# Attention, soft mixture of experts and MLP on one core: slot sums through a scaled stacking matrix, other early chunks of w_out, and single quarter copies of g

## The chip, the core and the metric

One Trainium2 chip, one core of it. The metric is the device time of one execution in microseconds (us). Engines: PE (TensorE), DVE (VectorE), ACT (ScalarE), POOL (GpSimd), SP (SyncE, which here issues the DMAs).

## What is computed

```python
attn_out = _attn_ref(q, k, v)            # 4 batches, 8 heads, 576 tokens, 64 wide; q and k rotated
x = attn_out.transpose(0, 2, 1, 3).reshape(2304, 512)
# soft mixture of experts, 32 slots
logits = x @ phi
d = exp(logits - logits.max(0)); d /= d.sum(0) + 1e-09     # over the tokens
slot_input = (d.T @ x).reshape(8, 4, 512)
for e in range(8):
    h = np.maximum(slot_input[e] @ w1[e], 0.0)             # 512 -> 1024
    slot_out[e] = h @ w2[e]                                # 1024 -> 512
c = exp(logits - logits.max(1)); c /= c.sum(1) + 1e-09     # over the slots
x = c @ slot_out
# MLP
h = x @ w_in                                               # 512 -> 2048
g = h * (1.0 / (1.0 + np.exp(-h)))
return g @ w_out                                           # 2048 -> 512
```

All of it is float32; matmuls of float32 go over PE in passes, or as sums of products of a high part and a low part (`_hi`, `_lo`).

## The kernel before

The work stands in four stages. Attention takes 16 pairs of heads one after the other. The mixture of experts keeps, while attention runs, a running slot sum `s_b` over the first three batches of tokens. The last batch is taken in two halves of 256 and 320 tokens: `half(0)` and `half(1)` return lists of functions (logits, maximum, exp, transposes, slot sums, merges), and the driver calls these, `h0[...]` and `h1[...]`, in an order written out by hand. `x_15(1)` transposes the last piece of x for the logits of half 1 (PE L414 and L416, ACT copy `xt` L418). Logits of half 1 come as four groups `lgh1` of eight passes (L514).

At the end of attention `sc` holds the factors by which older sums shrink when the maximum grows (ACT L538). The upper 64 rows of `s_b` are scaled on ACT (L539), the lower 64 are merged with the new sums on DVE (`merge` L568; two instructions of `slots`, L574). `slots` then multiplies `s_b` by the stacking matrix `stack_i`, which adds up the groups of 32 rows, into `si_ps` (PE L580) and copies it to `si` (DVE L581), in two rounds of 256 columns. Five small DVE operations make the slots' denominators `den`. The transposed logits `lt` (PE L842, DVE copies L844 and L845) serve the weights over slots. Layer 1 multiplies `si` by w1 (L871, 32 matmul groups of four for each half of its columns) and layer 2 by w2 (L892); the tiles `w` of both are loaded by SP. `slot_t(g)` copies a half of layer 2's result to SBUF as `o` (ACT L902) and transposes it to `so`.

The MLP folds w_in into the slots: `g_product(n)` multiplies `so` by a quarter of w_in (L1089; for the first columns L1126), and `gs` holds the result g spread over four groups of rows, as high and low parts. For n = 1 to 3 the spreading is done by `g_copy(n, r)`, r = 0 to 3, with four copies of 32x128 each; `ACT_QUADRANTS` says which of the four go to ACT (L1103), and the rest go to DVE (L1105). `hidden(j, k)` makes chunk k (128 columns of the 2048) for block j (768 of 2304 tokens): two matmuls `hps` (PE L1049), a sigmoid (ACT L1053), the product (DVE L1056), the high part `ghi` (ACT L1059) and the low part `glo` (DVE L1062). The products follow: for each of 3 blocks, 16 chunks and 6 groups of tokens three matmuls `ops` (L1154 to L1156).

The chunks of w_out arrive as 64-bit words and are narrowed to 32 bits by three instructions (ACT L134, DVE L137, DVE L140), then split into `wo_hi` (ACT L1031) and `wo_lo` (POOL L1032, or DVE where the call says so). Four chunks, `W_OUT_EARLY`, are loaded and narrowed during attention into `wf_early`. Of the others, 0 and 1 come ahead of the first products (tiles `wf_first`, `hw_first`), the rest within the products.

Order: all up to the split of chunk 1 is written out by hand under `tc.manual_schedule()`. Behind it, the framework's scheduler places the instructions, from the order of the code as a start. In the products, a table of steps (`G_STEPS`, step = 6 k + token group) says after which group of products the g products, copies and last conversions of w_in stand. The DMAs issued on SP take turns over 8 semaphores, and each waits for the landing of the eighth before it.

## Time and profile before

| | us |
|---|---|
| median of 3 runs | 573.48 (572.96 to 574.97) |
| the profiled execution | 573.27 |
| its span | 571.5 |
| PE busy | 540.4 (95%) |
| DVE busy | 316.9 (55%) |
| ACT busy | 307.9 (54%) |
| POOL busy | 111.3 (19%) |
| mean granted clock of PE | 0.982 |

The time is the span and 1.8 us around it. Times in rows are us from the start of the span. Attention ends at about 300, layers 1 and 2 run to 338, the MLP from there to the end. In a row of the timeline, the first number is the start, the second the duration (first to last end for a group), then engine, line, operation, what it writes and reads, sizes, and the count; in brackets stands how long the engine had been idle, and the instruction that ended that. The granted clock is given as a share of full speed.

### The profile page before, as it was taken

Reading aid. Unit: us, or ns where it says so; the run is one execution under the profiler, and the core shown is the slowest. Engines: PE = TensorE matmul, PEld = TensorE weight load, DVE = VectorE, ACT = ScalarE, POOL = GpSimd, SP = SyncE. Lnnn points to the kernel's source line nnn. Section 1 sums busy time; section 2 is a strip of 40 time slices with the busy share of each in tenths; the row PEclk is TensorE's granted clock in tenths of the full one; section 3 lists DMA queues with packets and bytes.
Section 4 is the critical chain, followed back from the end, with each engine's and each line's share of the span. In section 5 each row is a group of like instructions: output and inputs, shape, how many; then the busy total and the mean of one; then the engine's idle time right before and its main releaser. Section 6 shows DMA issues by size and latency. Waiting matters only on the chain.

```text
span 571.5 us, 15141 instructions
## 1 busy us (share of the span) xinstructions
PE 540.4 (95%) x6219; PEld 438.1 (77%) x6219; DVE 316.9 (55%) x841; ACT 307.9 (54%) x612; POOL 111.3 (19%) x96
## 2 busy tenths in 40 slices
PE   5599999999999999999979989899999999999997
PEld 2378989898897998888853337677888888888885
DVE  4756666766666567654130457697454444544442
ACT  2366667666767566664421327987554433544332
POOL 4933332313333323200000021133000000000000
PEclk9679999999999999999998999999999999999999
DMA  8226777635665575743799895422020000200003
GB/s 301 95 56 206 266 244 278 203 116 172 224 231 172 207 265 166 249 166 107 296 322 382 306 359 179 135 93 75 0 93 18 1 1 1 96 16 0 2 0 111
DMA packets 36773, 88.70 MB, mean 155 GB/s; under 512 B 10560, under 2 KB 11872, under 8 KB 34784
## 3 DMA queue, kind: packets, MB, share of 16 engines
q1 hardware_dynamic: 36694, 87.73, 44.3%
q8 instruction: 49, 0.80, 0.6%
q14 instruction: 20, 0.16, 0.1%
q10 hardware_dynamic: 10, 0.00, 0.0%
HBM read 78.20 MB, written 7.60 MB: 150 GB/s over the span
## 4 chain that ended last, share of the span: by engine, by line
PE 76%; ACT 10%; DVE 5%; DMA 4%; issue 3%; POOL 1%; SPq 1%; ACTq 0%; DVEq 0%
PE u L386 10%; PE ops L1156 10%; PE ops L1154 10%; PE ops L1155 10%; PE st L353 8%; PE psmx L300 3%; PE st_r L366 3%; PE l L871 3%; PE hps L1049 3%; ACT e L357 3%; PE xps L414 3%; DMA w_out_raw<-in_w_out_dram 2%; PE psmx L316 2%; ACT relu L308 2%; PE u L380 2%
## 5 line engine op out<-in xcount | busy, mean ns | idle before, releaser
L1056 DVE TENSOR_TENSOR hps<-hps,g 128x384 f32<-128x384 f32 x96 | 49.8, 561 | 84.6 <-ACT g L1053 84.3
L1053 ACT ACTIVATE g<-hps 128x384 f32<-128x384 f32 x96 | 42.3, 490 | 82.3 <-PE hps L1049 81.9
L1154 PE MATMUL ops<-wo_hi,ghi 128*128 128x512 f32 x216 | 84.7, 392 | 0.0
L1155 PE MATMUL ops<-wo_lo,ghi 128*128 128x512 f32 x216 | 84.4, 391 | 0.0
L1156 PE MATMUL ops<-wo_hi,glo 128*128 128x512 f32 x216 | 84.3, 390 | 0.0
L321 DVE CUSTOM_DVE_ANT_0 relu<-psmx,relu 128x288 f32<-128x288 f32 x140 | 57.7, 455 | 47.1 <-ACT e L357 36.3
L357 ACT ACTIVATE e<-st 128x512 f32<-128x512 f32 (+1 forms) x128 | 76.4, 650 | 10.9 <-PE st L353 10.9
L386 PE MATMUL u<-v,e 128*64 128x65 f32 x2048 | 80.6, 225 | 0.0
L386 PEld LDWEIGHTS u<-v,e 128*64 128x64 f32 x2048 | 71.5, 139 | 6.2 <-issue 3.0
L308 ACT ACTIVATE relu<-psmx 128x576 f32<-128x576 f32 x62 | 40.1, 652 | 51.7 <-PE psmx L300 33.6
L259 POOL TENSOR_TENSOR raw<-raw,tab 128x576 f32<-128x576 f32 x29 | 41.8, 1442 | 132.8 <-DMA raw<-in_qk_dram 96.7
L1062 DVE TENSOR_TENSOR glo<-hps,ghi 128x384 fp32r<-128x384 f32 x96 | 49.4, 552 | 5.0 <-ACT ghi L1059 1.8
L1059 ACT ACTIVATE ghi<-hps 128x384 fp32r<-128x384 f32 x96 | 45.6, 494 | 10.2 <-DVE hps L1056 10.1
L1156 PEld LDWEIGHTS ops<-wo_hi,glo 128*128 128x128 f32 x216 | 40.6, 188 | 8.5
L1155 PEld LDWEIGHTS ops<-wo_lo,ghi 128*128 128x128 f32 x216 | 40.6, 188 | 7.5 <-issue 0.4
L1154 PEld LDWEIGHTS ops<-wo_hi,ghi 128*128 128x128 f32 x216 | 40.6, 188 | 7.5 <-issue 0.2
L256 POOL TENSOR_TENSOR raw<-raw,tab 128x576 f32<-128x576 f32 x29 | 42.0, 1447 | 0.0
L353 PE MATMUL st<-hi 64*128 64x256 f32 (+1 forms) x256 | 39.7, 302 | 0.0
L353 PE MATMUL st<-mq,neg_a 64*128 64x256 f32 (+1 forms) x256 | 39.1, 297 | 0.6 <-DMA mq<-m 0.6
L353 PE MATMUL st<-hi,lo 64*128 64x256 f32 (+1 forms) x256 | 38.9, 296 | 0.0
L353 PE MATMUL st<-lo,hi 64*128 64x256 f32 (+1 forms) x256 | 38.9, 296 | 0.0
L397 DVE TENSOR_SCALAR r<-u 128x4 f32<-128x4 f32 (+1 forms) x32 | 5.2, 164 | 49.7 <-PE u L388 30.1
(223 smaller groups left out, 998.7 us busy)
## 6 DMA issues: line engine op xcount, KB each, us to landing
w<-in_w_dram SPq DMA_DIRECT2D x64, 512.0 KB
raw<-in_qk_dram SPq DMA_DIRECT2D x14, 1152.0 KB
w_out_raw<-in_w_out_dram SPq DMA_DIRECT2D x16, 512.0 KB
w_in_raw<-in_w_in_dram SPq DMA_DIRECT2D x12, 512.0 KB
v<-in_v_dram SPq DMA_DIRECT2D x16, 325.0 KB
out_dram<-os SPq DMA_DIRECT2D x18, 256.0 KB
raw<-in_qk_dram SPq DMA_DIRECT2D x4, 576.0 KB
w_in<-w_in SPq DMA_DIRECT2D x8, 256.0 KB
```

Source lines behind the costliest of these rows:

```text
L308: act.activation(out=r, in_=pair[:, :, 0:HS], func=ACTF.Relu)
L321: dve.tensor_tensor_reduce(out=r[:, hd], in0=t[hd], in1=r[:, hd], scale=1.0, scalar=-3.0e38, op0=ALU.add, op1=ALU.max, accum_out=mxs[p % 2 ...
L353: pe.matmul(st[:, hd, 0:n], lhsT=a, rhs=b, start=i == 0, stop=i == 3, skip_group_check=True)
L357: act.activation(out=e[:, :, 0:n], in_=st[:, :, 0:n], func=ACTF.Exp, scale=0.125)
L386: pe.matmul(u[q:q + 64, 2 * i + hd], lhsT=e[:, hd, o:o + 64], rhs=x[:, hd], start=n == 0 and i + hd == 0, stop=n == 4, skip_group_check=True)
L1053: act.activation(out=g[i], in_=t[i], func=ACTF.Sigmoid)
L1056: dve.tensor_tensor(out=t[i], in0=t[i], in1=g[i], op=ALU.mult)
L1059: act.activation(out=ghi[:, i], in_=t[i], func=ACTF.Copy)
L1062: dve.tensor_tensor(out=glo[:, i], in0=t[i], in1=ghi[:, i].bitcast(F32), op=ALU.subtract)
L1154: pe.matmul(t, lhsT=a, rhs=wo_hi[k], start=k == 0, stop=False)
L1155: pe.matmul(t, lhsT=a, rhs=wo_lo[k], start=False, stop=False)
L1156: pe.matmul(t, lhsT=b, rhs=wo_hi[k], start=False, stop=k == 15)
```

## The change

At the end of attention, `x_15(1)` moves from behind half 0's transposes to behind the first group of `lgh1`. The older sums `s_b` are no longer scaled in place: DVE scales the stacking matrix (`ss` = `stack_i` times `sc`), PE multiplies `s_b` by it, and adds the product of the newest sums with the plain `stack_i` in the same accumulators. For that, the newest sums are copied from PSUM to SBUF in two halves of 256 columns, one on ACT and one on DVE. One copy of 128x128 takes the place of two for `si`. The `lt` copies go to ACT, their accumulator into another pool, and the denominators (`total`) come last. `slot_t` copies its `o` in halves too. In both places, DVE's half waits for a semaphore of ACT in the built program, and the instruction that raises it is ACT's half of the same copy.

The early chunks of w_out are 0, 3, 6 and 10 instead of 3, 6, 9 and 12. So chunk 0's load and narrowing vanish from the start of the MLP, and its `wo_lo` is made on DVE there; 9 and 12 are now narrowed within the products. Two groups of products of chunk 0 are issued ahead of `g_spread`. The quarters of g are copied each at a step of its own, two of four on ACT instead of three, and the steps of the second and third g product and of the last conversion move.

```diff
-W_OUT_EARLY = (3, 6, 9, 12)
+W_OUT_EARLY = (0, 3, 6, 10)
...
-G_STEPS = (5, 7, 16, 19, 28, 14, 23, 37, 46, 53, 58)
-ACT_QUADRANTS = (0, 1, 2)
+G_STEPS = (5, 22, 52)
+LOAD_STEP = 28
+CONV_STEPS = (14, 23, 37, 44)
+ACT_QUADRANTS = (0, 1)
...
                         act.activation(out=sc[:, 5:6], in_=mall[:, 1:2], func=ACTF.Exp, bias=nmb[:, 5:6])
-                        act.activation(out=s_b[0][64:128], in_=s_b[0][64:128], func=ACTF.Copy, scale=sc[64:128, 5:6])
+                        ps["ss"] = p_r.tile([128, 3, NSLOT], F32, tag="dh0", name="ss")[:, 0]
+                        dve.tensor_scalar(out=ps["ss"], in0=stack_i[:, 0:NSLOT], scalar1=sc[:, 5:6], scalar2=None, op0=ALU.mult)
...
-                def slots():
-                    acc = s_b[0]
-                    for j in range(2):
-                        w = slice(256 * j, 256 * j + 256)
-                        dve.scalar_tensor_tensor(out=acc[0:64, w], in0=acc[0:64, w], scalar=sc[0:64, 5:6], in1=ps["s"][0:64, w], op0=ALU.mult, op1=ALU.add)
-                    t2 = ps_mx.tile([128, 2, 512], F32, tag="mx", name="si_ps")
-                    for j in range(2):
-                        t = t2[:, j]
-                        for k in range(2):
-                            c0 = 256 * j + 128 * k
-                            pe.matmul(t[:, NSLOT * k:NSLOT * k + NSLOT], lhsT=acc[:, c0:c0 + 128], rhs=stack_i[:, 0:NSLOT], start=True, stop=True)
-                        dve.tensor_copy(out=si[:, 2 * j:2 * j + 2], in_=t[:, 0:64].rearrange("p (k s) -> p k s", k=2))
+                def slots(t):
+                    o = hb[1][0:64, 0:DM]
+                    act.activation(out=o[:, 0:256], in_=ps["s"][0:64, 0:256], func=ACTF.Copy)
+                    dve.tensor_copy(out=o[:, 256:512], in_=ps["s"][0:64, 256:512])
+                    for k in range(4):
+                        pe.matmul(t[:, NSLOT * k:NSLOT * k + NSLOT], lhsT=s_b[0][:, 128 * k:128 * k + 128], rhs=ps["ss"], start=k == 0, stop=False, skip_group_check=True)
+                    for k in range(4):
+                        pe.matmul(t[:, NSLOT * k:NSLOT * k + NSLOT], lhsT=o[:, 128 * k:128 * k + 128], rhs=stack_i[0:64, 0:NSLOT], start=False, stop=True, skip_group_check=True)
+                    dve.tensor_copy(out=si, in_=t[:, 0:4 * NSLOT].rearrange("p (k s) -> p k s", k=4))
+
+                def total():
                     dve.tensor_tensor(out=scs[:, 3:5], in0=sc[:, 3:5], in1=sb[:, 3:5], op=ALU.mult)
...
-            h1[0]((0, 1, 2))
+            h1[0]((0,))
+            x_15(1)
+            h1[0]((1, 2))
             assert not tasks, tasks
             h0[3]()
             h0[5]()
-            x_15(1)
             h1[0]((3,))
             h1[2]()
             h0[4]()
             h1[3]()
+            h0[6]()
+            h0[8]()
+            h1[5]()
             h1[4]()
-            h0[6]()
-            h1[5]()
-            h0[8]()
+            t = ps_mx.tile([128, 2, 512], F32, tag="mx", name="lt3_ps")
             h1[6]()
-            t = ps_st.tile([128, 2, 512], F32, tag="st", name="lt3_ps")[:, 0]
+            h1[7](t[:, 1])
...
-            h1[7]()
-            dve.tensor_copy(out=lt[:, 15:19], in_=t[:, 0:4 * NSLOT].rearrange("p (c s) -> p c s", c=4))
-            dve.tensor_copy(out=lt[0:64, 19], in_=t[0:64, 4 * NSLOT:5 * NSLOT])
+            act.activation(out=lt[:, 15:19], in_=t[:, 0, 0:4 * NSLOT].rearrange("p (c s) -> p c s", c=4), func=ACTF.Copy)
+            act.activation(out=lt[0:64, 19], in_=t[0:64, 0, 4 * NSLOT:5 * NSLOT], func=ACTF.Copy)
+            h1[9]()
...
-            act.activation(out=o, in_=op[g], func=ACTF.Copy)
+            act.activation(out=o[:, 0:256], in_=op[g][:, 0:256], func=ACTF.Copy)
+            dve.tensor_copy(out=o[:, 256:512], in_=op[g][:, 256:512])
...
-        load_wo(0)
...
-            for k in range(2):
-                first.append((t[:, k], narrow(raw_w.pop(k), t[:, k], None, None, hw=h[:, k])))
+            first.append((t, narrow(raw_w.pop(1), t, None, None, hw=h)))
...
-        (wf0, _), (wf1, n1) = first
+        wf1, n1 = first[0]
+        split_hl(0, wf_early[0], dve)
...
-        hidden(*seq[0], between=lambda: (split_hl(0, wf0, dve), g_product(0)))
+        hidden(*seq[0], between=lambda: g_product(0))
         n1[0]()
+        for i in range(2):
+            products(0, 0, i, *gt[0, 0])
         g_spread()
...
+    for n in range(1, 4):
+        put(G_STEPS[n - 1], lambda n=n: g_product(n))
         for r in range(4):
-            g_copy(n, r)
...
+            put(NI * (4 * n + r - 3) + 1, lambda n=n, r=r: g_copy(n, r))
+    put(LOAD_STEP, lambda: load_last(1))
+    for k, x in enumerate(CONV_STEPS):
+        put(x, lambda k=k: conv_last(k))
```

DVE at the end of attention, before: `dh1` is the copy that the last slot sums wait for, `sps3` and `sps5` are the new sums of the halves.

```order
L530 TENSOR_SCALAR nmb_81<-mb_80,mall_85 128x1
L554 COPY dh1_4862<-dps5_4911 128x96
L568 SCALAR_TENSOR_TENSOR s_b0_77<-sps3_4902,sc_83,s_b0_77 64x512
L574 SCALAR_TENSOR_TENSOR s_b0_77<-s_b0_77,sc_83,sps5_4918 64x256 x2
L581 COPY si_79<-si_ps_4943 128x64 x2
L582 TENSOR_TENSOR scs_84<-sc_83,sb_82 128x2
```

The same place now (`last_logits_4826` is the buffer that now takes the newest sums):

```order
L532 TENSOR_SCALAR nmb_81<-mb_80,mall_85 128x1
L542 TENSOR_SCALAR ss_4900<-cst_sb_73,sc_83 128x32
L571 SCALAR_TENSOR_TENSOR s_b0_77<-sps3_4902,sc_83,s_b0_77 64x512
L557 COPY dh1_4862<-dps5_4912 128x96
L576 COPY last_logits_4826<-sps5_4920 64x256
L581 COPY si_79<-lt3_ps_4919 128x128
L584 TENSOR_TENSOR scs_84<-sc_83,sb_82 128x2
```

`ss` and the merge moved ahead of `dh1`; one half copy and one `si` copy replace two merges and two copies.

DVE at the start of the MLP, before: the numbers after `hps0_`, `ghi0_` and `glo0_` are the chunk and the half of its tokens.

```order
L908 COPY so_5035<-otp1_5334 128x4x16
L137 TENSOR_SCALAR wf_first_5322<-hw_first_5323 128x512
L140 SCALAR_TENSOR_TENSOR wf_first_5322<-w_out_raw0_5212,wf_first_5322 128x512
L929 TENSOR_TENSOR gs0_5343<-g0_ps_5373,gs0_5343 64x128
L1056 TENSOR_TENSOR hps0_0_0_5397<-hps0_0_0_5397,g0_0_0_5401 128x384
L1056 TENSOR_TENSOR hps0_0_1_5399<-hps0_0_1_5399,g0_0_1_5404 128x384
L1032 TENSOR_TENSOR wo_lo0_5408<-wf_first_5322,wo_hi0_5407 128x512
L1062 TENSOR_TENSOR glo0_0_5396<-hps0_0_0_5397,ghi0_0_5395 128x384
L1062 TENSOR_TENSOR glo0_0_5396<-hps0_0_1_5399,ghi0_0_5395 128x384
L929 TENSOR_TENSOR gs0_5343<-g0_all_5435,gs0_5343 64x384
L137 TENSOR_SCALAR wf_first_5322<-hw_first_5323 128x512
L140 SCALAR_TENSOR_TENSOR wf_first_5322<-w_out_raw1_5217,wf_first_5322 128x512
```

The same place now:

```order
L907 COPY o1_5334<-l2_1_5240 128x256
L1033 TENSOR_TENSOR wo_lo0_5372<-wf_early_903,wo_hi0_5371 128x512
L913 COPY so_5038<-otp1_5337 128x4x16
L934 TENSOR_TENSOR gs0_5343<-g0_ps_5377,gs0_5343 64x128
L1057 TENSOR_TENSOR hps0_0_0_5401<-hps0_0_0_5401,g0_0_0_5405 128x384
L1057 TENSOR_TENSOR hps0_0_1_5403<-hps0_0_1_5403,g0_0_1_5408 128x384
L1063 TENSOR_TENSOR glo0_0_5400<-hps0_0_0_5401,ghi0_0_5399 128x384
L1063 TENSOR_TENSOR glo0_0_5400<-hps0_0_1_5403,ghi0_0_5399 128x384
L934 TENSOR_TENSOR gs0_5343<-g0_all_5443,gs0_5343 64x384
L139 TENSOR_SCALAR wf_first_5324<-hw_first_5325 128x512
L139 TENSOR_SCALAR wf2_5480<-hwo2_5481 128x512
L142 SCALAR_TENSOR_TENSOR wf_first_5324<-w_out_raw1_5218,wf_first_5324 128x512
```

Chunk 0's narrowing is gone from between `so` and `gs0`, its `wo_lo0` stands ahead of `so`, and a step of chunk 2 has come between the two steps of chunk 1.

ACT in the products, at the first g product of the four that are spread by copies, before: `gh1` and `gl1` are its high and low part.

```order
L1095 ACTIVATE gh1_5536<-g_ps1_5519 128x128
L1103 ACTIVATE gs0_5343<-gh1_5536 32x128 x2
L1103 ACTIVATE gs0_5343<-gl1_5537 32x128
L1103 ACTIVATE gs0_5343<-gh1_5536 32x128 x2
L1103 ACTIVATE gs0_5343<-gl1_5537 32x128
L1103 ACTIVATE gs0_5343<-gh1_5536 32x128 x2
L1103 ACTIVATE gs0_5343<-gl1_5537 32x128
L1103 ACTIVATE gs0_5343<-gh1_5536 32x128 x2
L1103 ACTIVATE gs0_5343<-gl1_5537 32x128
L1053 ACTIVATE g0_3_0_5573<-hps0_3_0_5571 128x384
L1053 ACTIVATE g0_3_1_5580<-hps0_3_1_5578 128x384
```

The same place now:

```order
L1096 ACTIVATE gh1_5536<-g_ps1_5519 128x128
L1054 ACTIVATE g0_3_0_5561<-hps0_3_0_5559 128x384
L1104 ACTIVATE gs0_5343<-gh1_5536 32x128 x3
L1054 ACTIVATE g0_3_1_5568<-hps0_3_1_5566 128x384
L1104 ACTIVATE gs0_5343<-gh1_5536 32x128 x2
L1060 ACTIVATE ghi0_3_5557<-hps0_3_0_5559 128x384
L1104 ACTIVATE gs0_5343<-gh1_5536 32x128
L1060 ACTIVATE ghi0_3_5557<-hps0_3_1_5566 128x384
L136 ACTIVATE hwo5_5650<-w_out_raw5_5489 128x512
L136 ACTIVATE hw3_1_5706<-w_in_raw3_0_5228 128x512
L1054 ACTIVATE g0_4_0_5615<-hps0_4_0_5613 128x384
L1032 ACTIVATE wo_hi4_5605<-wf4_5600 128x512
```

Twelve copies in a row became eight (six of them here), which stand in groups among the sigmoids and high parts of the next chunks.

## Rows read from the trace of the kernel before

**Rows 1.** The page, part 4: shares of the chain that ended last.

```profile
PE 76%; ACT 10%; DVE 5%; DMA 4%; issue 3%; POOL 1%; SPq 1%; ACTq 0%; DVEq 0%
```

**Rows 2.** Stretches: length, busy PE, PEld, DVE, ACT, POOL, granted clock, DMA share, GB/s.

```profile
296.70:300.60 3.90, 1.77 (x17) 1.42 (x14) 2.35 (x11) 0.00 (x0) 0.00 (x0) 1.00 0.76 237
300.60:304.90 4.30, 4.30 (x25) 1.42 (x29) 0.00 (x0) 0.00 (x0) 0.00 (x0) 0.60 1.04 393
301.50:304.60 3.10, 3.10 (x20) 1.04 (x16) 0.00 (x0) 0.00 (x0) 0.00 (x0) 0.50 1.06 404
323.00:340.00 17.00, 15.48 (x130) 6.25 (x126) 4.89 (x15) 3.49 (x9) 0.57 (x1) 1.00 1.02 395
373.00:400.00 27.00, 25.91 (x141) 20.75 (x141) 22.80 (x47) 20.80 (x48) 9.28 (x6) 1.00 0.25 79
```

**Rows 3.** Timeline, the logits of half 1 and the last transposes of x.

```profile
288.65 1.82 PE L514 MATMUL lgh<-xt,phi_sb 128*32 128x320 f32 x24
...
289.67 0.47 ACT L533 ACTIVATE last_logits<-lgh,nmb 128x256 f32<-128x256 f32 x1 [2.41 <-DVE mall L527]
...
291.46 0.44 ACT L418 ACTIVATE xt<-xps 128x320 f32<-128x320 f32 x1 [1.04 <-PE xps L416]
...
291.95 0.75 PE L514 MATMUL lgh<-xt,phi_sb 128*32 128x320 f32 x8 [0.54 <-ACT xt L418]
```

**Rows 4.** Timeline, a half copy on ACT, then the slot sums up to layer 1.

```profile
286.87 0.39 ACT L516 ACTIVATE last_logits<-lgh 128x256 f32<-128x256 f32 x1 [2.39 <-PE lgh L511]
...
294.12 0.28 ACT L538 ACTIVATE sc<-mall,nmb 128x1 f32<-128x1 f32 x1
...
294.86 0.26 DVE L554 COPY dh<-dps 128x96 f32<-128x96 f32 x1 [1.35 <-PE dps L552]
295.03 0.73 DVE L568 SCALAR_TENSOR_TENSOR s_b<-sps,sc,s_b 64x512 f32<-64x512 f32 x1
...
296.91 0.87 DVE L574 SCALAR_TENSOR_TENSOR s_b<-s_b,sc,sps 64x256 f32<-64x256 f32 x2 [1.14 <-PE sps L565]
...
300.60 0.64 PE L871 MATMUL l<-w,si 128*32 128x512 f32 x4 [1.58 <-DVE lt L845]
```

**Rows 5.** Timeline of layers 1 and 2: first matmuls, last weight loads, last matmuls.

```profile
300.60 12.20 PE L871 MATMUL l<-w,si 128*32 128x512 f32 x96 [1.58 <-DVE lt L845]
...
303.41 18.83 SPq L120 DMA_DIRECT2D w<-in_w_dram  x16
...
336.17 1.94 PE L892 MATMUL l<-w,ht 128*32 128x512 f32 x16
```

**Rows 6.** Timeline, the start of the MLP.

```profile
338.23 0.60 ACT L902 ACTIVATE o<-l 128x512 f32<-128x512 f32 x1 [5.27 <-PE l L892]
...
339.43 4.37 POOL L1032 TENSOR_TENSOR wo_lo<-wf_early,wo_hi 128x512 fp32r<-128x512 f32 x3 [22.65 <-DMA w_in<-w_in]
...
341.02 1.64 DVE L140 SCALAR_TENSOR_TENSOR wf_first<-w_out_raw,wf_first 128x512 uint32<-128x512 uint32 x1
342.69 0.29 DVE L929 TENSOR_TENSOR gs<-g_ps,gs 64x128 fp32r<-64x128 f32 x1
...
347.45 0.43 DVE L137 TENSOR_SCALAR wf_first<-hw_first 128x512 uint32<-128x512 uint32 x1
...
347.91 0.69 DVE L140 SCALAR_TENSOR_TENSOR wf_first<-w_out_raw,wf_first 128x512 uint32<-128x512 uint32 x1
...
350.63 0.39 PE L1154 MATMUL ops<-wo_hi,ghi 128*128 128x512 f32 x1
```

**Rows 7.** Timeline of the first stall; groups of 347 to 400 (count, busy, mean ns, idle).

```profile
361.77 0.45 PE L1049 MATMUL hps<-cs,gs 128*128 128x384 f32 x1 [1.16 <-DVE glo L1062]
...
L1049 PE MATMUL hps<-cs,gs 128*128 128x384 f32 x22 | 7.5, 370 | 2.4 <-DVE glo L1062 1.8 <-DVE gl L1096 0.5
L1103 ACT ACTIVATE gs<-gh 32x128 fp32r<-32x128 f32 x22 | 6.8, 309 | 0.3
...
L1105 DVE CAST gs<-gl 32x128 fp32r<-32x128 f32 x12 | 2.7, 222 | 0.2
```

More of the change, by code (lines that the diff above doesn't have):

```diff
@@ L586, in slots @@
                     dve.reciprocal(out=den, in_=den)
-                return logits, logits2, soft, expo, keep, d_t, s_mm, slots, merge
+                return logits, logits2, soft, expo, keep, d_t, s_mm, slots, merge, total
             CHUNKS = [[(128 * c, min(128, S - 128 * c)) for c in range(5)]] * 4
@@ L992, in t3 @@
             combine_t(3)
-            t, h = (wa.tile([128, 2, 512], F32, tag=f"w{i}", name=n) for i, n in ((3, "wf_first"), (4, "hw_first")))
-            for k in range(2):
-                first.append((t[:, k], narrow(raw_w.pop(k), t[:, k], None, None, hw=h[:, k])))
+            t, h = (wa.tile([128, 512], F32, tag=f"w{i}", name=n) for i, n in ((3, "wf_first"), (4, "hw_first")))
+            first.append((t, narrow(raw_w.pop(1), t, None, None, hw=h)))
         first = []
@@ L999, in attn_softmoe_mlp_kernel @@
         slot_t(1)
-        for f in first[0][1]:
-            f()
         gs2 = [spare(10, "gs0")]
@@ L1113, in attn_softmoe_mlp_kernel, with products @@
     seq = [(j, k) for j in range(NBLK) for k in range(16)]
+    ops = {}
+    def products(j, k, i, ghi, glo):
+        if k == 0:
+            ops[j, i] = ps_o.tile([128, DM], F32, tag="o", name=f"ops{j}_{i}")
+        t = ops[j, i]
+        a, b = ghi[:, 128 * i:128 * i + 128], glo[:, 128 * i:128 * i + 128]
+        pe.matmul(t, lhsT=a, rhs=wo_hi[k], start=k == 0, stop=False)
+        pe.matmul(t, lhsT=a, rhs=wo_lo[k], start=False, stop=False)
+        pe.matmul(t, lhsT=b, rhs=wo_hi[k], start=False, stop=k == 15)
     def dummy(n):
@@ L1136, in attn_softmoe_mlp_kernel, with put @@
     hidden(*seq[1])
-    def copies(n):
-        for r in range(4):
-            g_copy(n, r)
-    extra = {}
-    for x, f in zip(G_STEPS, (lambda: g_product(1), lambda: copies(1), lambda: g_product(2), lambda: copies(2), lambda: load_last(1),
-                              lambda: conv_last(0), lambda: conv_last(1), lambda: conv_last(2), lambda: conv_last(3), lambda: g_product(3), lambda: copies(3))):
-        extra.setdefault(divmod(x, 6), []).append(f)
-    ops = {}
+    extra = {}
+    def put(x, f):
+        extra.setdefault(divmod(x, NI), []).append(f)
+    for n in range(1, 4):
+        put(G_STEPS[n - 1], lambda n=n: g_product(n))
+        for r in range(4):
+            put(NI * (4 * n + r - 3) + 1, lambda n=n, r=r: g_copy(n, r))
+    put(LOAD_STEP, lambda: load_last(1))
+    for k, x in enumerate(CONV_STEPS):
+        put(x, lambda k=k: conv_last(k))
     for n, (j, k) in enumerate(seq):
@@ L1149, in attn_softmoe_mlp_kernel @@
         for i in range(NI):
-            if k == 0:
-                ops[j, i] = ps_o.tile([128, DM], F32, tag="o", name=f"ops{j}_{i}")
+            if (j, k, i) not in ((0, 0, 0), (0, 0, 1)):
+                products(j, k, i, ghi, glo)
             t = ops[j, i]
-            a, b = ghi[:, 128 * i:128 * i + 128], glo[:, 128 * i:128 * i + 128]
-            pe.matmul(t, lhsT=a, rhs=wo_hi[k], start=k == 0, stop=False)
-            pe.matmul(t, lhsT=a, rhs=wo_lo[k], start=False, stop=False)
-            pe.matmul(t, lhsT=b, rhs=wo_hi[k], start=False, stop=k == 15)
             if (n, i) in extra:
```

2 lines of the change are left out of this document (1 added, 1 removed).

## The prediction

> **What bounds the kernel now.** I read the chain of waits first: PE carries 76% of it, ACT 10%, DVE 5% [rows 1]. So the end moves only where PE waits or runs at a lower clock. The edit touches two places where that happens: the stretch between the last attention matmuls and layer 1, and the start of the MLP with its first products. Next I took busy time and granted clock by stretch. In 296.7 to 300.6 PE works 1.77 of 3.90 us. Right after that, in layer 1, the granted clock is 0.50 for 3.1 us, that is 1.2 GHz, and 0.60 on the mean over 300.6 to 304.9, where PE has no gap at all [rows 2]. Then I went through the timeline at the end of attention [rows 3, 4], layer 1 [rows 5] and the start of the MLP [rows 6], and last the waits of the hidden matmuls in the products [rows 7]. All sums are made against the profiled execution, 573.27 us, which is 0.21 under the median of 573.48.
>
> **A, the end of attention.** Three edits lie one behind the other here.
>
> *x_15 earlier.* Before, PE ran 24 logit matmuls from 288.65, waited for the exp of half 0, ran the 12 passes that transpose x, then waited for ACT's copy of them (291.46, 0.44 us) before the last eight logit passes at 291.95 [rows 3]. Now the transposes stand after the first eight (0.6 us), so they run by 290.2, under no wait. ACT's copy precedes the exp instead of following it: copy 290.05 to 290.5, exp 0.47 plus its accumulator read to 291.15, dps matmuls 0.3, last logits at about 291.4. That is 0.5 to 0.6 earlier. The new queue position costs the exp 0.8, but what waits for the exp (dps) was not what ended last.
>
> *The older slots' scaling and the merge go ahead of dh1 on DVE.* Before, dh1 (294.86) came first and the merge of 0.73 after it [rows 4]. Now ss, a 128x32 operation (0.15 to 0.20 by the small DVE rows: the 128x96 copy is 0.26), and the merge are queued ahead. They begin when sc is ready, 294.4 unshifted, so dh1 is copied at 295.2 to 295.3, which is 0.35 to 0.45 late, and the last slot-sum matmuls wait for exactly that. Both together: −0.2.
>
> *Slots.* Before, DVE starts its two merges at 296.91 and layer 1 starts at 300.60: 3.69 us through two merges, si matmuls, a copy, si matmuls again, a copy, five small DVE operations for den, and the two lt copies on which layer 1's tile waited (1.58 us of PE idle on DVE) [rows 4]. Now the four products with ss run at once, 0.86 us for eight passes at layer 1's 10.5 / 96 [rows 5], and hidden behind the copies. The 64x256 half copy on ACT takes 0.39 as its 128x256 one does [rows 4]. DVE's half waits for ACT's, so the two stand in a row: 0.8, and the products with the last two column groups come behind it. From PE's end of sps5 (296.8): 0.8 of copies, 0.45 for the last four passes, 0.2 drain, 0.27 for the si copy, and PE takes the lt transposes (0.47) beside that. Layer 1 no longer waits for den or lt copies, only for si: about 299.4. That is −1.2, between −0.6 if ss, the copies and semaphores each take 0.15 more, and −1.6.
>
> A = −0.2 − 1.2 = **−1.4** (−0.8 to −1.8). Two weight loads gated by the new matmuls start 0.75 later. The last of these loads is issued at 322.24, at most eight are in flight, and at 395 GB/s each 0.52 MB takes 1.33 us: all landed by 332.9, against their use at 336.17 [rows 2, 5]. So 3.3 us of lead cover the 3.1 us that A and B take out.
>
> **B, the clock.** The granted clock fell 0.9 us into layer 1, after the 3.90 us in which PE had worked 1.77 [rows 2]. At 0.60 over 4.3 us PE loses 0.40 × 4.3 = 1.7 us, and the 96 passes of the first group take 12.20 instead of about 10.5 [rows 5]. After the change the stretch is one third shorter and holds more: 16 si passes instead of 8, so some 2.1 us of work in 2.7. The other stretch with gaps in these rows, 323 to 340, has 15.48 us of work in 17.00 and keeps 1.00 [rows 2]; the new stretch lies between the two, and much shorter. I take the gain whole: B = **−1.7**, the other end 0.
>
> **C, the start of the MLP.** The o copy of slot_t was one ACT instruction of 0.60 at 338.23 [rows 6]. Two halves in a row are 0.39 + 0.40: +0.2. Then chunk 0's narrowing is gone from DVE, whose long member (1.64) held the g split until 342.69. Without that step only ACT's half of the split stands ahead of it, so g comes some 1.4 earlier, 1.1 after paying the 0.2 and a little of so's wait, and ghi with it. But chunk 1 takes most of it back. On DVE its second narrowing step (347.91, 0.69) now stands behind an extra step of chunk 2 (0.43 as its own first step at 347.45), which waits for ACT's step on that chunk, and six product matmuls (1.4 us) precede g_spread on PE. Chain: step two at about 348.7, hps of k = 1 behind it, ghi at 350.4, products of k = 1 at about 350.5, where they began at 350.63 [rows 6]. C = **−0.1**: −1.4 if chunk 1 does not gate, +0.5 if its row of waits is 0.15 longer at each of four steps.
>
> **D, the first stall in the products.** Before, ACT took 12 quarter copies in a row behind gh1. At 0.309 each (the group's 22: 6.8 us) [rows 7] they hold the sigmoid of k = 3 for 3.7. PE then waits 1.16 for glo at 361.77 [rows 7]. Now the quarters come one by one between the sigmoids and eight of the twelve stay on ACT, so its run in front of a sigmoid is three copies, 0.9, not twelve. But DVE gets four casts more per product at 0.222 [rows 7], and chunk 4's and w_in's steps move ahead. I leave 0.3 of the 1.16 standing: D = **−0.9**, between −0.3 (two of the three parts of the wait come back as casts ahead of glo) and −1.2 (all of it gone).
>
> **E, later stalls.** Hidden matmuls wait on glo 1.8 in all and on gl 0.5 in 347 to 400 [rows 7]; without the 1.16 of D, 1.2 is left. Single quarters take out most of it. Against it stand, on DVE, 12 casts (2.7) and one more late chunk (0.69 + 0.43 = 1.1). DVE is busy 22.80 of 27.0 in 373 to 400 [rows 2], so of its 4.2 idle some 2 remain: full but not over. E = **−0.3**, between −1.2 (all of it) and +0.8 (two new stalls of 0.4).
>
> Sum: −1.4 − 1.7 − 0.1 − 0.9 − 0.3 = −4.4. 573.27 − 4.4 = **568.9**, 0.8% under the median.
>
> **A rule against the trace.** In rows 6 a DVE step with two operands in SBUF took 1.64 beside POOL's three wo_lo in a row (339.43, 4.37), and 0.69 without POOL. The Trainium skill (SBUF — State Buffer, section "🔬 SBUF: two separate sides") states that such a DVE operation and a GpSimd one exclude each other, that the first to start holds the ports for its whole instruction and the other blocks. By that rule, the trace agrees: 1.64 − 0.69 = 0.95 of blocking. The change puts chunk 0's wo_lo on DVE right there, beside POOL's three. By the rows it is lost only if POOL starts first. ACT makes wo_hi0 before wo_hi3, about 0.6 apart, so DVE starts first and POOL waits: the sum stays −4.4, against −3.5 with POOL first.
>
> **The rivals.**
>
> *The clock falls all the same.* Then B is 0 and the rest stands: 573.27 − 2.7 = **570.6**. For it: these rows show one fall only, so how thin PE's work must be is not known, and PE still waits 0.8 for the copies and some 0.5 for si. Against it: the work in the gap grows while the gap shrinks by a third. Chance 0.2.
>
> *DVE's wo_lo0 comes behind POOL.* It then takes 1.64, so goes to g, and from there to ghi 0.95 later: −4.4 + 0.95, **569.9**. Chance 0.08.
>
> *Chunk 1 does not gate.* C is −1.4: **567.6**. It needs ACT's step on chunk 2 to be done before DVE asks, and PE's six early groups to hold g_spread up less than their 1.4. Chance 0.1.
>
> *DVE becomes the bound of the products, slower than before.* Its queue now mixes casts and narrowing steps between hps and glo. When a late chunk's 1.1 us stands ahead of a glo, PE waits as at 361.77, 1.16 each. Eleven chunks pass. At the fourth such stall (4.6) the gain is gone; at six (7.0) the time is 573.27 − 4.4 + 7.0 = **575.9**. For it: DVE's idle share there falls to 2 in 27. Against it: a glo is only asked for one k later, and six PE groups of 0.7 us lie between. Chance 0.05.
>
> **How the numbers follow.** Forecast 0.57, clock 0.2, POOL first 0.08, chunk 1 free 0.1, DVE bound 0.05. A measurement of this kernel tells 0.3% from no change, 1.7 us: faster is under 571.8, slower over 575.2. Faster: nearly all of the forecast's, three quarters of the clock rival's, all of the next two: 0.86. Same, from the tails of forecast and clock rival: 0.09. Slower: 0.05. Range: low end from chunk 1 free with the other terms' gains at part of their bounds, 566.8; high end from the clock rival with E at its bad end, 570.6 + 1.1 = 571.7. Beyond them lie some 0.1 on each side.
>
> **What would show it.** A: layer 1 starts at about 299.2 (300.60), with PE's wait ended by the si copy. B: a granted clock of 1.00 in the 4 us from layer 1's start, and its 96 passes in 10.5. C: first products some 1.1 earlier, those of k = 1 at the same distance behind layer 2 as before. D and E: the hidden matmuls' waits on glo and gl fall from 2.3 to about 1.2 by 400. Wrong if layer 1 again runs at 0.50, if the products' waits on DVE grow over 2.4, or if layer 2 waits for weights.

## The result and the profile after the change

The changed kernel takes **576.07 us** (median; 574.45 to 580.35 in 20 runs) beside 573.22 of the kernel before on the same chip: a ratio of 1.0051, between 1.0034 and 1.0067. It is slower, by 2.9 us, where 4.6 less was forecast, and outside the range. The profiled execution took 576.25, its span 574.5.

First the page of the kernel after, its head and its part 4, the shares of the chain that ended last; PE has gone from 76% to 75% and DVE from 5% to 7% [rows 1].

```profile
span 574.5 us, 15150 instructions
...
PE 75%; ACT 7%; DVE 7%; DMA 5%; issue 4%; POOL 1%; ACTq 0%; SPq 0%; DVEq 0%; POOLq 0%
```

Then milestones of the two timelines (start times in us from the span's start). "Product n" is the n-th of the 864 product matmuls `ops`, so that at each milestone both kernels have the same products behind them; "hps of k" below is the first hidden matmul of the k-th chunk.

| milestone | before | after | after − before | of it new | step |
|---|---|---|---|---|---|
| first logits of half 1 | 286.14 | 285.14 | −1.00 | −1.00 | ahead of the change |
| layer 1, first pass | 300.60 | 298.50 | −2.10 | −1.10 | A |
| layer 1, 96th pass | 312.22 | 308.42 | −3.80 | −1.70 | B |
| layer 2, last group of 16 passes | 336.17 | 334.05 | −2.12 | **+1.68** | not forecast |
| product 19, the first of k = 1 | 350.63 | 348.47 | −2.16 | −0.04 | C |
| product 82, second g product done in both | 371.05 | 370.16 | −0.89 | **+1.27** | D |
| product 172 | 396.82 | 400.18 | +3.36 | **+4.25** | E |
| end of the span | 571.5 | 574.5 | +3.0 | −0.4 | E |

Counting products matters here. The k-th hidden matmul does not stand behind the same work in both kernels: at hps of k = 1, k = 5 and k = 11, 8, 67 and 171 products are done before the change and 12, 63 and 171 after it, and the second g product stands ahead of hps of k = 5 only before. By equal work, D is +1.3 and E is 4.25 − 0.37 = +3.9: from product 19 to the end the changed kernel takes **5.2 us more**, and the loss begins in the stretch of D.

The first row is no effect of the edit: in the 14 executions profiled for this case the first logits of half 1 begin between 283.79 and 286.50, after different times in the start-up, and kernels that share all code up to there differ as much. Differences are therefore taken between milestones, never from the start.

The end of the attention and layer 1 went as described. Timeline of the kernel after (start, length, instruction, idle before it and what ended that):

```profile
295.82 0.38 ACT L575 ACTIVATE last_logits<-sps 64x256 f32<-64x256 f32 x1 [2.56 <-PE sps L568]
296.23 0.42 DVE L576 COPY last_logits<-sps 64x256 f32<-64x256 f32 x1 [2.21 <-ACT last_logits L575]
296.65 1.07 PE L580 MATMUL lt_ps<-cst_sb,last_logits 64*128 64x32 f32 x8
297.76 0.29 DVE L581 COPY si<-lt_ps 128x128 f32<-128x128 f32 x1 [1.12 <-PE lt_ps L580]
298.50 4.07 PE L875 MATMUL l<-w,si 128*32 128x512 f32 x36
```

Copies in a row, products, one si copy, then layer 1: the chain of two merges and two lt copies in rows 4 is gone. Three stretches of the kernel after, with the columns of rows 2:

```profile
298.50:303.00 4.50, 4.50 (x46) 1.46 (x48) 0.39 (x3) 0.35 (x2) 0.00 (x0) 1.00 0.97 323
...
360.00:373.00 13.00, 11.18 (x77) 8.57 (x76) 12.68 (x24) 8.85 (x23) 4.25 (x3) 1.00 0.48 162
373.00:400.00 27.00, 22.66 (x120) 16.59 (x119) 25.19 (x46) 18.72 (x42) 9.43 (x7) 1.00 0.29 99
```

The first 4.5 us of layer 1 have a granted clock of 1.00 where rows 2 had 0.60. But in 373 to 400 DVE is busy 25.19 of 27 (22.80 before) and PE only 22.66 (25.91 before): PE is busy 3.25 us less in a stretch where its clock is 1.00 in both. The timeline of PE there lists who ended its waits, nearly all of them glo:

```profile
363.18 0.44 PE L1050 MATMUL hps<-cs,gs 128*128 128x384 f32 x1 [1.08 <-DVE glo L1063]
...
367.29 1.08 PE L1090 MATMUL g_ps<-w_in_n,so 128*32 128x128 f32 x32 [0.73 <-DVE glo L1063]
...
375.54 0.44 PE L1050 MATMUL hps<-cs,gs 128*128 128x384 f32 x1 [1.12 <-DVE glo L1063]
...
386.69 0.91 PE L1050 MATMUL hps<-cs,gs 128*128 128x384 f32 x2 [0.76 <-DVE glo L1063]
...
392.89 0.90 PE L1050 MATMUL hps<-cs,gs 128*128 128x384 f32 x2 [1.20 <-DVE glo L1063]
...
397.09 1.08 PE L1090 MATMUL g_ps<-w_in,so 128*32 128x128 f32 x32 [0.79 <-DVE glo L1063]
```

As a group of 347 to 400 (columns of rows 7), the hidden matmuls wait 4.8 us where they waited 2.4:

```profile
L1050 PE MATMUL hps<-cs,gs 128*128 128x384 f32 x19 | 7.6, 407 | 4.8 <-DVE glo L1063 4.6
```

DVE has more to do there, 113 instructions between hps of k = 0 and of k = 13 where the kernel before has 100. But some of its steps also take far longer than the same steps elsewhere, and the runs below show that this is what costs the time. Two pairs from the timeline, POOL's low part of a late chunk and the DVE step that starts 0.22 and 0.11 us behind it, then a pair in which nothing is lost:

```profile
373.54 1.28 POOL L1033 TENSOR_TENSOR wo_lo<-wf,wo_hi 128x512 fp32r<-128x512 f32 x1 [2.25 <-ACT wo_hi L1032]
373.76 1.14 DVE L1106 CAST gs<-gl 32x128 fp32r<-32x128 f32 x1
...
386.91 1.28 POOL L1033 TENSOR_TENSOR wo_hl<-wf,wo_hl 128x512 fp32r<-128x512 f32 x1 [1.29 <-ACT wo_hl L1032]
387.02 1.45 DVE L139 TENSOR_SCALAR wf<-hwo 128x512 uint32<-128x512 uint32 x1
...
351.90 1.30 POOL L1033 TENSOR_TENSOR wo_lo<-wf,wo_hi 128x512 fp32r<-128x512 f32 x1 [10.53 <-ACT wo_hi L1032]
352.23 1.02 DVE L1063 TENSOR_TENSOR glo<-hps,ghi 128x384 fp32r<-128x384 f32 x2 [0.28 <-ACT ghi L1060]
```

The cast takes 1.14 against 0.222 [rows 7], the narrowing step 1.45 against 0.43 [rows 6], and they end 0.08 and 0.28 us behind POOL (374.82 and 388.19). The two glo of the last pair, which read `hps` in PSUM, take the 0.55 each that they take everywhere; so do the products of `hps` beside POOL. I call a step blocked when it took at least 0.4 us longer than the shortest of its line and shape. Between hps of k = 0 and of k = 13 there are 8 of them, casts and narrowing steps alone, with 8.36 us in excess; the kernel before has 2 with 1.89.

And layer 2 is longer. Its last matmuls before the change, then after, then in the run e4 below, which has no warm-up matmul there:

```profile
320.30 1.94 PE L892 MATMUL l<-w,ht 128*32 128x512 f32 x16
322.17 0.70 PE L1118 MATMUL warm<-cst_sb 128*128 128x256 f32 x2
322.80 5.41 PE L892 MATMUL l<-w,ht 128*32 128x512 f32 x48
```

```profile
316.56 1.93 PE L896 MATMUL l<-w,ht 128*32 128x512 f32 x12
318.42 0.70 PE L1130 MATMUL warm<-cst_sb 128*128 128x256 f32 x2
319.05 7.05 PE L896 MATMUL l<-w,ht 128*32 128x512 f32 x52
```

```profile
315.88 7.14 PE L896 MATMUL l<-w,ht 128*32 128x512 f32 x64
```

By these rows, four passes of 128x32 on four different tiles take the time of one: 7.14 for 64 is 0.45 per four. Before, the warm-up stood behind the fourth of four tiles, 16 passes. After, it stands behind the third: 12 passes take the 1.93 of 16, and 52 take 7.05, the time of 64. The tile that was cut off runs alone: the last four of the 52 start 0.43 apart (324.22 to 325.51), the others in fours within 0.05. 7.05 + 1.93 against 5.41 + 1.94 is 1.63 of the 1.68 us. In the code the warm-up's place did not change; the scheduler, which fills layer 2, put it there.

### The profile page after: what moved, and what is told of

Its sections match the earlier page's. It is cut to its first block, busy times and chain, and to the rows that moved or that the text cites. A ratio compares the mean times of both kernels' runs of the same rounds, so it can differ in the third digit from the quotient of the medians.

```text
span 574.5 us, 15150 instructions
## 1 busy us (share of the span) xinstructions
PE 542.4 (94%) x6227; PEld 437.9 (76%) x6227; DVE 323.3 (56%) x852; ACT 303.8 (53%) x602; POOL 109.9 (19%) x96
## 4 chain that ended last, share of the span: by engine, by line
PE 75%; ACT 7%; DVE 7%; DMA 5%; issue 4%; POOL 1%; ACTq 0%; SPq 0%; DVEq 0%; POOLq 0%
PE u L388 10%; PE ops L1123 10%; PE ops L1125 10%; PE ops L1124 10%; PE st L355 8%; PE psmx L302 3%; PE st_r L368 3%; PE hps L1050 3%; ACT e L359 3%; PE xps L416 3%; PE l L875 2%; PE psmx L318 2%; ACT relu L310 2%; DMA w_in_n<-w_in 2%; PE u L382 2%
```

## The experiments

All on the same chip type, each beside runs of the kernel before. The last two columns are from the profiles: "products" is how much more than in the kernel before lies between product 19 and the end of the span, and the last counts the blocked DVE steps as above, with their excess (us). The runs were made on several chips, where the kernel before had medians of 572.59 to 573.84; a difference of two medians of this table carries that with it, a ratio does not.

| run | median | ratio to before (95%) | products | blocked, excess |
|---|---|---|---|---|
| after | 576.07 | 1.0051 (1.0034, 1.0067) | +5.2 | 8, 8.36 |
| e1 copies of g back | 571.92 | 0.9975 (0.995, 1.0) | +0.1 | 3, 2.52 |
| e2 three of four on ACT | 573.69 | 0.9998 (0.9975, 1.0022) | +2.6 | 3, 2.62 |
| e3 no POOL | 569.18 | 0.9919 (0.9897, 0.994) | −2.1 | 0 |
| e4 no warm-up | 573.76 | 0.9999 (0.9981, 1.0016) | +4.4 | 7, 7.30 |
| e5 = e1 + e4 | 569.6 | 0.9938 (0.9915, 0.9962) | +0.1 | 3, 2.51 |
| e6 attention only | 571.65 | 0.9961 (0.9942, 0.998) | −0.2 | 2, 1.89 |
| e7 quarters only | 572.18 | 0.9962 (0.9944, 0.998) | −0.6 | 5, 3.49 |
| e8 early set 0, 8, 10, 12 | 573.77 | 1.0011 (0.9985, 1.0037) | +2.6 | 6, 5.77 |
| e9 first quarters single | 572.46 | 0.9992 (0.9973, 1.0012) | +3.6 | 4, 2.83 |
| e10 before, no POOL | 572.83 | 1.0002 (0.9978, 1.0025) | +0.2 | 0 |
| e11 whole copies | 573.43 | 1.0021 (0.9996, 1.0045) | +4.7 | 8, 7.16 |
| e12 MLP only | 577.24 | 1.006 (1.0039, 1.0082) | +4.4 | 7, 7.28 |

The loss goes with the blocked time, not with the number of DVE's instructions. Four profiles hold some 1.6 or 1.7 of low clock in the products (e2, e4, e9, e11, given below). Without that, up to 3.5 us of blocked time goes with 2.0 or less, and 5.8 to 8.4 with 2.6 to 5.2. e11 has 101 DVE instructions between hps of k = 0 and of k = 13, one more than the kernel before, and loses; e7 has 112 and gains.

**Three theories of what the products lost,** numbered as in the expectations. 1: the copies of g fill DVE, with twelve casts more, single and late. 2: the one more late chunk fills DVE. 3: POOL's low parts hold DVE's steps up, some 1.1 us each time. The first three runs bear on them.

**e1: the copies of g in a row, as before, with three of each four on ACT.**

```
-G_STEPS = (5, 22, 52)
+G_STEPS = (5, 16, 53)
...
-CONV_STEPS = (14, 23, 37, 44)
-ACT_QUADRANTS = (0, 1)
+CONV_STEPS = (14, 23, 37, 46)
+ACT_QUADRANTS = (0, 1, 2)
...
-            put(NI * (4 * n + r - 3) + 1, lambda n=n, r=r: g_copy(n, r))
+            put((7, 19, 58)[n - 1], lambda n=n, r=r: g_copy(n, r))
```

> The changed kernel with the copies of g as before: all four quarters of a product at one step (7, 19, 58), three of four on ACT, g products at 5, 16, 53, last conversion at 46. Theory 1 (the copies fill DVE: twelve casts more, single and late): the loss of 8.3 us between k = 5 and k = 11 goes back to under 2, time about 570. Theory 2 (one more late chunk, five in a row behind chunk 10, fills DVE): the loss stays above 5, time 573 to 576. Theory 3 (POOL's wo_lo blocks DVE about 1.1 us each time): the loss falls only by the blocked casts, by 2 to 3, time 573 to 574.

It measured 571.92. The products' +5.2 goes to +0.1: the loss is gone. D's gain does not come either, since from product 19 to 82 it takes 0.8 more than in the kernel before. By the size of the step this is what theory 1 said, and more than theory 3 gave; but the blocked steps fell too, from 8 to 3, and e1 changes the place and the number of the copies and the steps of two g products and a conversion at once. It cannot part theory 1 from theory 3. (The profiled execution took 575.59, the longest of the eight, for a clock that is told under B below.)

**e2: only ACT's share of the copies.**

```
-ACT_QUADRANTS = (0, 1)
+ACT_QUADRANTS = (0, 1, 2)
```

> The changed kernel with three of four quarters on ACT; steps as changed. Theory 1: DVE has 12 casts less (2.7 us), and the loss between k = 5 and k = 11 falls by 2.7 or more, time 572 to 573.5. Theories 2 and 3: it falls by 0 to 2, time 574 to 576.

573.69, a part: twelve casts given back from DVE to ACT take 2.4 off the 576.07, between what theory 1 and the other two said. Its products lose 2.6, of which some 1.7 is a granted clock of 0.83 over 390 to 400 (0.17 × 10). Here too the blocked steps fell to 3.

**e3: POOL does not make the late chunks' low parts.**

```
-        eng.tensor_tensor(out=wo_lo[k], in0=w, in1=wo_hi[k].bitcast(F32), op=ALU.subtract)
+        if eng is pool and k not in wf_early:
+            wo_lo[k] = wo_hi[k]
+        else:
+            eng.tensor_tensor(out=wo_lo[k], in0=w, in1=wo_hi[k].bitcast(F32), op=ALU.subtract)
```

> The changed kernel without the low parts of w_out for the late chunks (POOL's wo_lo is left out for them and the products read wo_hi instead, so that part of the sum is another). The order on DVE and ACT is that of the changed kernel, word for word. Theory 3: eight DVE instructions between k = 3 and k = 11 that took 1.0 to 1.2 longer than their like come back to 0.22, 0.42 and 0.69; 8 x 1.1 = 8.8 us of DVE time, most of the loss of 8.3 gone, time 568 to 570. Theories 1 and 2: DVE is over full without POOL too, the loss falls by less than 3, time 573 to 576.

This leaves out work that the result needs, so it is a probe and no version. 569.18, that is 6.9 under the changed kernel, with DVE's and ACT's instructions in the same order. The groups of DVE and of the hidden matmuls from hps of k = 5 on, first of the kernel after (363 to 400), then of e3 (361 to 392); columns: count, busy time and mean ns of one, idle before:

```profile
L142 DVE SCALAR_TENSOR_TENSOR wf<-w_out_raw,wf 128x512 uint32<-128x512 uint32 x9 | 8.5, 939 | 0.2
...
L1106 DVE CAST gs<-gl 32x128 fp32r<-32x128 f32 x15 | 6.2, 414 | 0.3
...
L139 DVE TENSOR_SCALAR wf<-hwo 128x512 uint32<-128x512 uint32 x8 | 5.4, 680 | 0.2
...
L1050 PE MATMUL hps<-cs,gs 128*128 128x384 f32 x13 | 5.2, 409 | 4.6 <-DVE glo L1063 4.6
```

```profile
L142 DVE SCALAR_TENSOR_TENSOR wf<-w_out_raw,wf 128x512 uint32<-128x512 uint32 x9 | 6.2, 689 | 0.2
...
L1109 DVE CAST gs<-gl 32x128 fp32r<-32x128 f32 x15 | 3.3, 221 | 0.3
...
L139 DVE TENSOR_SCALAR wf<-hwo 128x512 uint32<-128x512 uint32 x8 | 3.4, 425 | 0.3
...
L1053 PE MATMUL hps<-cs,gs 128*128 128x384 f32 x13 | 4.4, 376 | 0.3 <-DVE glo L1066 0.2
```

The same 32 DVE instructions take 20.1 us with POOL's steps and 12.9 without, and the waits on glo go from 4.6 to 0.2. This decides for theory 3: the count and the order of DVE's instructions are the same, only their lengths changed. PE's waits in the changed kernel were not for POOL itself: between product 1 and hps of k = 11 none of over 0.1 us ended with a `wo_lo` of POOL. Without the blocking the products take 2.1 less than in the kernel before (−0.7 up to product 82, −1.4 behind it), so the single quarters and the earlier chunks bring what D and E hoped for (−1.2), and more. Theories 1 and 2 name what brings the steps beside POOL, not the loss itself.

**e10: the same cut in the kernel before.** It asks whether the blocking costs time of itself (the diff is that of e3).

> The kernel before without POOL's low parts for its late chunks (the products read wo_hi instead, so that part of the sum is another); order on DVE as before. There two DVE instructions are blocked, 1.9 us in all. Theory 3 as a matter of room (a blocked instruction costs time only where DVE has none left): the time falls by 0 to 2, to 571.5 to 573.5, against 6.9 in the changed kernel. If POOL's blocking cost the same everywhere per instruction on the chain, or POOL cost PE something by itself, it would fall by 4 or more.

572.83 against 572.59, and +0.2 in the products: nothing. (Its profile also has a granted clock of 0.54 over 342.9 to 346.5, 1.6 us that lie ahead of product 19.) Its two blocked steps were gone, and so were waits of 0.29 for glo and 0.55 for gl; but two others for glo, 0.40 and 0.15 in the kernel before, were 0.93 and 1.28 here, so nothing came of the faster steps. Two blocked steps cost nothing in the kernel before; eight cost the changed kernel 7 us.

**e4: no warm-up matmul, the line `dummy(1)` taken out.**

> The changed kernel without the single warm-up matmul (two passes), which the scheduler puts into layer 2, now behind the third instead of the fourth weight tile of a group of four. If it splits the groups so that one tile of the next ones runs alone (4 passes x 0.43 in place of 0.107), layer 2 ends 1.6 + 0.6 earlier against layer 1's start, and the time falls by 1.6 to 2.2, to about 574. If the stretch was lost to weight transfers, it stays at 576 within 0.7.

573.76, 2.3 under the changed kernel, and layer 2, from its first to its last pass, is 19.59 long where the changed kernel has 21.98. That it is even shorter than before the change (20.30) is the 0.70 of the warm-up.

**e5: e1 and e4 together.**

> The two repairs at once: copies of g as before the change, and no single warm-up matmul in layer 2. If the two losses are separate and add, the median is the 571.9 of the first less 1.6 to 2.2, about 570, so faster than both kernels (before: 573.5). If DVE is what bounds from k = 6 on whatever comes ahead, it stays at 571.5 to 572.5.

569.6, a ratio of 0.9938: under both kernels. Its hidden matmuls in 344 to 392, where the kernel after has 4.8:

```profile
L1050 PE MATMUL hps<-cs,gs 128*128 128x384 f32 x20 | 7.0, 374 | 2.5 <-DVE glo L1063 2.5
```

2.5 is what the kernel before has (2.4): this version keeps A and B, has no cut layer 2, and gives the products' gain and loss up.

**e6 and e12: the two halves of the change.** e6 is the kernel before with the edits of the attention alone (x_15, ss, slots, total, lt copies); e12 has all edits of the MLP and none of those.

> The kernel before with the end of attention of the changed one alone (x_15 earlier, ss, half copies, lt copies on ACT); MLP as before. Its warm-up matmul too stands behind the third tile of the four. Expected by the parts measured so far: layer 1 starts 1.1 earlier against the last logits, the clock holds in most executions (1.7 to 2), layer 2 gives 1.6 back to the split groups: 573.5 - 1.4 = about 572, with a granted clock of 0.984 or 0.985 in most runs instead of 0.979 to 0.982. If the clock's gain was chance, the clocks spread as before and the time is 573.5 to 574.

> The kernel before with the MLP part of the change alone (early chunks 0, 3, 6, 10, half copies of o, products ahead of g_spread, single quarters); end of attention as before. In the MLP, DVE and ACT run in the changed kernel's order, word for word, and the warm-up matmul stands behind the fourth tile as before. If the two halves of the change add, it is the changed kernel's 576.1 plus the attention part's 2 that is missing: about 578, with eight or so blocked DVE instructions and 8 us lost between k = 5 and k = 11. If the loss came from the earlier start of the MLP (weights or transfers not there yet), it shrinks, to 575 or less.

571.65 and 577.24. The loss of the products is in the MLP's half (+4.4 in e12). The gain of A and B is in the attention's, and the long layer 2 too: 21.97 in e6, while e12 has the warm-up behind the fourth tile. In e6 the terms give −1.1 − 1.7 + 1.7 = −1.1, where −2.1 was measured; the interval of its ratio reaches from −1.1 to −3.3, so the sum lies at its edge, and no run shows where the rest comes from. The start of layer 1 in e6, then in e12:

```profile
299.30:304.30 5.00, 5.00 (x50) 1.59 (x52) 0.39 (x3) 0.35 (x2) 0.00 (x0) 1.00 0.96 337
```

```profile
299.00:305.00 6.00, 4.71 (x29) 1.59 (x33) 1.01 (x7) 0.00 (x0) 0.00 (x0) 0.72 1.02 382
```

**e7: single quarters alone, on the kernel before; e8: another early set, with 8, 10 and 12 beside chunk 0, on the kernel after.**

```
+    for n in range(1, 4):
+        put(G_STEPS[n - 1], lambda n=n: g_product(n))
+        for r in range(4):
+            put(NI * (4 * n + r - 3) + 1, lambda n=n, r=r: g_copy(n, r))
```

```
-W_OUT_EARLY = (0, 3, 6, 10)
+W_OUT_EARLY = (0, 8, 10, 12)
```

> The kernel before with the changed copies of g alone: single quarters, two of four on ACT, g products at 5, 22 and 52, last conversion at 44; early chunks 3, 6, 9 and 12 as before. Theory 1 with 3 (casts fill DVE and push its narrowing in front of POOL's wo_lo): first stall goes (about 2 to 3.5 gained by k = 5), then 5 to 8 lost by k = 11, at least five blocked DVE instructions, time 575 to 578. Theory 2 (the early set is at fault): no more than two or three blocked, time 570.5 to 573.

> The changed kernel with chunks 0, 8, 10 and 12 early instead of 0, 3, 6 and 10; the number of late chunks is the same, but behind k = 6 only 7, 9, 11, 13, 14 and 15 are late, and ahead of it 3 and 6 more. Theory 2 (too many late chunks in a row behind 10): the loss of 8.3 between k = 5 and k = 11 falls below 4, though some comes back earlier, time 571 to 574. Theory 1 with 3: DVE has the same work, the loss moves forward, time 575 to 577.

e7 measured 572.18, 1.6 under the kernel before, with 0.6 less in the products: single quarters alone pay, though five steps are blocked, for 3.49. Time and count came out as different theories said. e8 measured 573.77, in the range of theory 2, with +2.6 where the changed kernel has +5.2; but six steps are still blocked. So the early set and the quarters make the loss together: the quarters alone −0.6, the early set with the copies in a row +0.1 (e1), both +5.2.

**e9 and e11: two ways to improve on e5.** Shown is what differs from e5, in e11 the second of the two copies. e9 takes the first g product's quarters one by one; e11 makes the copies of sps and o whole, on ACT.

```
-            put((7, 19, 58)[n - 1], lambda n=n, r=r: g_copy(n, r))
+            put((7 + 6 * r, 19, 58)[n - 1], lambda n=n, r=r: g_copy(n, r))
```

```
-            act.activation(out=o[:, 0:256], in_=op[g][:, 0:256], func=ACTF.Copy)
-            dve.tensor_copy(out=o[:, 256:512], in_=op[g][:, 256:512])
+            act.activation(out=o, in_=op[g], func=ACTF.Copy)
```

> The two repairs, with the first spread g product alone copied by single quarters (steps 7, 13, 19, 25; three of four on ACT), the second and third in a row as before. If single quarters pay where DVE still has room, the first stall shrinks by 2 to 3 as it did with quarters on the kernel before, and nothing comes back behind k = 6: 569.6 - 2.5 = about 567. If they only move the work into the later, fuller stretch, it stays at 569 to 570.5.

> The two repairs, with whole copies on ACT in place of halves on ACT and DVE (newest slot sums 64x512, o 128x512). The halves stand in a row (0.38 + 0.42), a whole copy takes 0.60: by that, layer 1 starts 0.2 earlier and each transposition of o is 0.1 to 0.2 earlier, 569.6 - 0.4. If the halves let the first products begin sooner and that counts, the time is 0.2 to 0.5 longer. Either is read from the profile, the time alone cannot tell it.

Both missed: 572.46 and 573.43. In e11 the edit itself is nearly free: from the last logits to layer 1 it takes 7.70 with whole or half copies, and from layer 2's last pass to the first product 6.93 instead of 6.71. The loss is in the products, which the edit does not touch in the code. There some 25 rows of DVE's order differ from e5's, since the scheduler planned anew, 8 steps are blocked for 7.16 us instead of 3 for 2.51, and 1.7 of the +4.7 is a clock of 0.83 in 370 to 380. In e9 50 rows differ, and of its +3.6 a clock of 0.84 in 390 to 400 makes up 1.6. An edit that is worth 0.2 us at its place moved the products by 3, the clock left out.

## Why the prediction was wrong, step by step

**A** held in the profile of the kernel after: −1.1 where −1.4 stood, inside its bounds. Layer 1 waits for si alone, and starts 7.70 behind the last logits of half 1.

**B** held there: −1.7 as taken, from the clock and nothing else. It is not had in every execution. The mean clock of a whole execution is a check on many of them: e6, whose products are those of the kernel before, has 0.984 or 0.985 in 11 of 11, and the kernel before has 0.982 or less in 29 of 30 on the same chip (86 of 96 on four chips). The kernel after has 0.984 or 0.985 in 17 of 20. But of the ten profiles with this edit, those of e1, e2 and e8 show the fall in layer 1; and in e1 and e2 the clock falls once more ahead of it, so that layer 1 starts 9.26 and 9.25 behind the last logits and A is lost too. e1, at the last slot sums and from layer 1's start:

```profile
296.00:298.00 2.00, 2.00 (x25) 1.45 (x21) 0.03 (x1) 0.38 (x1) 0.00 (x0) 0.50 0.31 119
...
300.60:305.00 4.40, 4.40 (x31) 1.29 (x33) 0.44 (x3) 0.35 (x2) 0.00 (x0) 0.62 0.97 344
```

What decides it in an execution stays open.

**C** held: from the last group of layer 2 to the first products of k = 1 it takes 14.42 (14.46 before), though the very first products come 1.8 earlier. Chunk 1 does take it back. One part had the wrong sign: the half copies of o, costed at +0.2, gain 0.22 over a whole copy (e5 against e11), since the first two transposes start behind ACT's half.

**The lead of the weights** held: no matmul of layer 2 waited for a load. But layer 2 was taken as untouched by A and B, and it is not: +1.68, by the place of the warm-up. I read the order of the engines only where the diff names code. The cut of the tiles stood in the order of the changed kernel; what was missing was its price, which rows of the kernel before come near: 16 of these passes in 1.94, 0.12 each [rows 5], beside 0.39 for a single 512-column matmul [rows 6].

**D** did not come: from product 19 to 82 the changed kernel takes 1.3 more, where −0.9 stood. The reasoning on ACT's copies was right: in e3, with the same order, the stretch takes 0.7 less, and the wait of 1.16 at k = 4 is down to 0.08 in the kernel after too. But a wait of 1.08 for glo stands ahead of k = 5 in its place and one of 0.73 ahead of the second g product, and both are gone in e3. Ahead of the first, a narrowing step of DVE is held up by POOL:

```profile
360.29 1.29 POOL L1033 TENSOR_TENSOR wo_lo<-wf,wo_hi 128x512 fp32r<-128x512 f32 x1 [7.09 <-ACT wo_hi L1032]
360.35 1.52 DVE L139 TENSOR_SCALAR wf<-hwo 128x512 uint32<-128x512 uint32 x1
```

**E is the step that failed,** and it took D with it. It said "full but not over", with 2 us of DVE's idle left, and counted casts and narrowing steps at the durations that they have alone. In the products these lie beside POOL's low parts, and there they take about 1.0 us longer (0.9 to 1.1) where POOL started first. In the kernel before this happened twice, and it cost nothing, as e10 shows. In the changed kernel it happened eight times, 8.4 us of DVE, and came out as six waits for glo of 0.73 to 1.20 and one of 0.40: E is +3.9 where −0.3 stood, D and E together +5.2 where −1.2 stood, and without the blocking (e3) they would be 7.3 shorter. The fourth rival, with a chance of 0.05, named the right engine and very nearly the right waits, six of 1.16. It missed why they come: its price is close to one blocked step, and a late chunk's 1.1 us of work is there in e3 too, without the waits. That its 575.9 lies so near 576.07 is in part luck, for it holds nothing of layer 2's 1.7.

The rule that was weighed was the right rule at the wrong place. By the rows, wo_lo0 at 337.06 took 0.69 with POOL's three right behind it at 337.62:

```profile
337.06 0.69 DVE L1033 TENSOR_TENSOR wo_lo<-wf_early,wo_hi 128x512 fp32r<-128x512 f32 x1
...
337.62 3.75 POOL L1033 TENSOR_TENSOR wo_lo<-wf_early,wo_hi 128x512 fp32r<-128x512 f32 x3 [24.64 <-ACT wo_hi L1032]
```

DVE was first, as forecast, and nothing was lost there. The Trainium skill (SBUF — State Buffer, section "🔬 SBUF: two separate sides") states that a DVE operation in a two-port mode, or with two inputs in SBUF, and a GpSimd one exclude each other, and that the first to start holds the shared ports for its whole instruction. By that rule, the traces agree: 1.64 and 1.45 of a step of 0.69 and 0.43 behind POOL, no loss ahead of it, and none in e3. I applied it to the one instruction that the change moved to DVE, and not to the late chunks, whose low parts POOL makes all through the products while the change moves DVE's casts and narrowing steps among them.

**The sum.** −1.10 (A), −1.70 (B), +1.68 (layer 2), −0.04 (C), +1.27 (D), +3.88 (E): +4.0 in the profiled executions, and with −1.0 ahead of the change the +3.0 of the spans. With D and E as forecast and layer 2 untouched it would have been −4.0, near the forecast's −4.4.

What stays open: how the loss of the products divides between the early set and the casts, since with most edits of the products the scheduler plans them anew; and why the five blocked steps of e7 cost nothing, while four in e9 go with a loss.

## What to carry to other kernels

When an engine is said to be "full but not over", count its steps at the length that they have beside their neighbours, not alone: here each cast or narrowing step of DVE that POOL held up paid about 1.0 us, which cost nothing in the kernel before, with two of them, and 6.9 us in the changed one, with eight. Read the order of the whole stretch that a scheduler plans, not only of the lines in the diff; one unrelated warm-up between column tiles cost 1.6 us, and a change of two copies moved the products by 3. Measure a stretch between two points that have the same work behind them: by the k-th hidden matmul, D would have looked like a gain. And test the parts of a change by themselves: the attention half (0.9961) and the single quarters (0.9962) each pay alone, and the whole loses.
